# RetNet recurrence and gated MLP on one core: in the last period but one, both chunks' score products in one run, their result products in another, and one split of their rows

## The chip, the cores and the metric

The kernel runs on one core of a Trainium2 chip. The metric is the device time of one execution in microseconds (us), smaller is better. Three runs of the kernel before took 612.45, 612.64 and 613.05 us, so its median is 612.64 us. TensorE is called PE in the profile, its weight loads PEld, VectorE DVE, ScalarE ACT, GpSimd POOL and SyncE SP. PEq or SPq is an engine's sequencer, where DMAs are issued and semaphores are waited for.

## The reference, cut to what matters

```python
# attention: batch 4, 8 heads, 768 steps, head size 64; gamma has one value for each head
for t in range(S):
    state = gamma * state + outer(k[:, :, t], v[:, :, t])
    y[:, :, t] = scale * (q[:, :, t] @ state)
x = y as (3072, 512)
# MLP: w_in is 512 x 2048, w_out 2048 x 512
h = x @ w_in
g = h * erf(softplus(h))
out = g @ w_out
```

## The kernel before, in words

**Rows.** The 3072 rows are cut into 24 chunks of 128 rows, and two chunks make a group of 256, so there are 12 groups (`NG`, 0 to 11). A batch entry has 6 chunks. The recurrence is computed chunk by chunk, with half chunks of 64 rows inside, and the state is handed from half chunk to half chunk.

**One chunk of the recurrence** is made of five steps:

- `begin` (line 560): the scores, 16 products of 64x64 (line 566), and what the halves add to the state, 16 such products, or 8 for the last chunk of a batch entry, which hands on no state from its second half (line 573). A product of this size leaves two records in the trace, so these are 32 and 32 (or 16) records. The results lie in two banks of PSUM.
- `states` (line 578): on DVE, two maskings of the scores (line 582) and one or two additions to the state (line 593).
- `results` (line 595): 16 products of the states with the queries (line 611) and 16 of the masked scores with the values (line 622), into two banks; then two copies of them to the rows of x on ACT (line 630).
- `crossed_sums` (line 633): two additions on DVE (line 641) of what one half chunk owes to the other.
- `split_x` (line 643): the rows of x are split for the products in the reduced fp32 format, into hi, lo and dif (`split`, line 311: one instruction on ACT, line 314, and two on DVE, lines 315 and 316). The three go to one of three places of a ring, `XR`.

`prepare` (line 531) has transposed and scaled the queries, keys and values of two chunks some units earlier, in five steps: three on DVE, and two of eight scalings on ACT (line 550).

**The hidden layer.** Line 720 (`pair_unit`) multiplies one column block of w_in with the rows of two groups: a *unit* is 8 products of hi and lo into a first bank and 4 of dif into a second, all 128x128 weights against 512 columns. After it, `put` combines the two banks (`together`, line 320: line 322 on ACT, which reads the first bank, and line 323 on DVE, which reads the second) and sends the result to DRAM from POOL (line 731). Two sets of banks, o0/o1 and o2/o3, take turns.

**Periods.** The loop at line 1000 runs over periods `g`. `period` (line 936) gives for each the eight units, what TensorE does ahead of a unit (the first dictionary, called `pe` in the loop) and what is issued after it (the second, `other`). The order of issue for each unit is thus: `pe`, the unit's products, `other`, `put`. The order is written out by hand, and every engine works off its queue in that order. In period `g` the chunks `2g + 2` and `2g + 3` go through the recurrence, and the units multiply groups that are complete. In period 10 (`NG - 2`) these are chunks 22 and 23, and the units are those of groups 9 and 10; chunk 23 is the last of its batch entry and has the 8 products at line 573. Period 11 is the first that reads the rows of group 11 (chunks 22 and 23), from its unit 0 on. There four sets of banks take turns (r, hp, o0/o1, o2/o3).

Most periods (5 to 9 among them, line 961, and a like one at line 950) take what the helper `joined` (line 925) gives: `begin` of both chunks ahead of one unit, and `results` of both ahead of another, the first chunk in the two banks of pool `ps_h` (named hp), the second in the two of `ps_r` (named r). There `begin` stands ahead of unit 2 and `results` ahead of unit 5.

Period 10 has its own order (line 972): the four runs of small products stand ahead of units 1, 2, 3 and 5, `begin` in `ps_h` and `results` in `ps_r`. Its other work is the first of w_out: `load_w_out` (line 869, issued on SP) and `split_w_out` (line 876: line 306 on ACT, lines 307 and 308 on DVE), the load of the hidden layer back from DRAM (`load_hidden`, line 841, on SP), and `softplus`, `erf` and `gated` (lines 846, 850, 860) for the first rows.

**The output layer.** After period 12 line 905 (`project`) multiplies g with w_out, 128x128 against 512 columns, group by group. Even groups use the banks r and hp, odd ones the o banks.

Of the kernel before, what the change touches and what calls it, by code (L numbers as in the profile page):

```python
# [49 lines left out]
def kernel(  # L50
# [747 lines left out]
    a, b = JPC, JPC + 1  # L798
# [126 lines left out]
    def joined(at, to, g):  # L925

        a, b = 2 * g + 2, 2 * g + 3
        return {
            at: [(begin, a, ps_h), (begin, b, ps_r)],
            to: [(results, a, None, ps_h), (results, b, None, ps_r)],  # L930
        }
# [4 lines left out]
    def period(g, prep, next_prep):  # L936

        a, b = 2 * g + 2, 2 * g + 3
        one, two = partial(partial, unit), partial(partial, pair_unit)
        if g == G2:  # L940
            units = [one(g, n) for n in range(NPC // 2)]
            return units, {0: [(results, a), (results, b, None, ps_h)]}, {
                0: [(crossed_sums, a), (crossed_sums, b)],
                1: [(split_x, a, 2)],
                2: [(split_weights, 4)],
                3: [(steps, next_prep, 4)],
            }, range(4)
        if g < NG:
            units = [two(g - 1, ft) for ft in range(8 * (g % 2), 8 * (g % 2) + 8)]
        if g == G2 + 1:  # L950
            return units, joined(2, 5, g), {
                0: [(steps, prep)],
                1: [(split_weights, 5)],
                2: [(states, a), (states, b)],
                3: [(split_weights, 6)],
                4: [(split_weights, 7)],
                5: [(crossed_sums, a), (crossed_sums, b)],
                6: [(split_x, a, 2)],
                7: [(steps, next_prep, 1)],
            }, range(4)  # L960
        if g < NG - 2:
            return units, joined(2, 5, g), {
                0: [(steps, prep, 4)],
                1: [(convert, 2)],
                2: [(states, a), (convert, 1)],
                3: [(states, b), (convert, 1)],
                4: [(convert, 2 if g < 8 else 1)],
                5: [(crossed_sums, a), (crossed_sums, b)],
                6: [(split_x, a, 2)],
                7: [(steps, next_prep, 1 if g < NG - 3 else 4), (convert, 1)],  # L970
            }, LOADS.get(g, ())
        if g == NG - 2:
            return units, {1: [(begin, a)], 2: [(results, a)], 3: [(begin, b)], 5: [(results, b)]}, {
                0: [(steps, prep, 4), (load_w_out, 0)],
                1: [(states, a), (load_w_out, 1)],
                2: [(crossed_sums, a), (split_w_out, 0)],
                3: [(states, b), (split_x, a)],
                4: [(split_w_out, 1), (load_hiddens, 0)],
                5: [(crossed_sums, b)],
                6: [(split_x, b), (softplus, 0), (load_w_out, 2)],  # L980
                7: [(erf, 0), (gated, 0)],
            }, ()
        if g == NG - 1:
            return units, {}, {
                0: [(split_g, 0), (split_w_out, 2), (load_w_out, 3)],
                1: [(split_g, 1), (load_hiddens, 1)],
                2: [(split_w_out, 3)],
                3: [(softplus, 1), (load_w_out, 4)],
                4: [(erf, 1)],
                5: [(split_w_out, 4), (load_w_out, 5)],  # L990
                6: [(gated, 1)],
                7: [(split_g, 2), (load_hiddens, 2)],
            }, ()
        return [one(NG - 1, n) for n in range(NPC // 2)], {}, {
            0: [(split_w_out, 5), (load_w_out, 6)],
            1: [(split_g, 3), (load_w_out, 7)],
            2: [(split_w_out, 6)],
        }, ()

    for g in range(G2, NG + 1):  # L1000
        pair = load_pair(2 * g + 4) if 2 * g + 4 < NJ else iter(())
        next_prep = prepare(2 * g + 4) if 2 * g + 4 < NJ else iter(())
        units, pe, other, loads = period(g, prep, next_prep)
        for i, work in enumerate(units):
            for f, *args in pe.get(i, ()):
                f(*args)
            put = work()
            steps(pair, 3)
            for part in itertools.islice(quarters, loads.count(i)):
                load_quarter(part)  # L1010
            if g == NG - 1 and i % 2:
                W.pop(NPC // 2 + i // 2)
            if g == NG:
                W.pop(i)
            for f, *args in other.get(i, ()):
                f(*args)
            put()
            while behind:
                behind.pop(0)()
        prep = next_prep  # L1020
    split_w_out(7)

    for n in range(NG * NU):
        g, i = divmod(n, NU)
# [62 lines left out]
```

## Time and profile before

| | |
|---|---|
| median of three runs | 612.64 us (612.45 to 613.05) |
| the profiled execution | 613.15 us |
| its span, from the first instruction to the last | 611.40 us |
| around the span | 1.75 us |
| PE busy | 604.6 us, 99% of the span |
| PEld busy | 507.3 us, 83% |
| DVE busy | 459.8 us, 75% |
| ACT busy | 390.3 us, 64% |
| granted TensorE clock | 1.000 |
| period 10, from its unit 0 to unit 0 of period 11 | 286.01 to 313.05 us of the span |

A row of the timeline reads: start in us, length in us, engine, line, operation, the tile written and the tiles read, shapes, and xcount, where several records are merged. In brackets stands how long the engine was idle before it and what ended the wait. Matmuls are pipelined: a large one is listed with 0.39 us though the next starts 0.23 us later. The distance between starts is therefore what a piece of work costs PE, not the listed length.

### The profile page before, as it was taken

What the parts mean: (1) busy time and instruction counts of PE and PEld (TensorE: products, weight loads), DVE (VectorE), ACT (ScalarE), POOL (GpSimd) and SP (SyncE); (2) the same over time, 40 slices, a digit from 0 to 9 for tenths busy, and PEclk for the clock granted to TensorE, in tenths of its full rate; (3) what the DMA queues carried; (4) which work ended last, traced back from release to release, by engine and by line L of the source; (5) the groups of instructions that cost most, each with busy time, mean ns of one, the idle gap of its engine ahead of it and who ended that gap; (6) DMA issues with size and microseconds to landing.
All of it is one profiled execution on the core that took longest, in us unless ns stands there. A gap on an engine that the chain in (4) does not pass through costs nothing.

```text
span 611.4 us, 13214 instructions
## 1 busy us (share of the span) xinstructions
PE 604.6 (99%) x5222; PEld 507.3 (83%) x5222; DVE 459.8 (75%) x581; ACT 390.3 (64%) x614; POOL 132.5 (22%) x228
## 2 busy tenths in 40 slices
PE   8999999999999999999999999999999999999997
PEld 7888889888888888888788988888888888888886
DVE  5899988886978679787768978686776768668640
ACT  3667446354453634345387699889789888988920
POOL 1087435443526535241112200000000000000000
PEclk9999999999999999999999999999999999999999
DMA  9999659977979998894645834325324333531300
GB/s 203 312 263 281 149 132 248 265 161 221 219 201 277 269 270 182 243 233 151 215 143 187 286 119 148 127 70 173 103 88 154 106 129 110 172 119 55 103 35 34
DMA packets 143949, 106.28 MB, mean 174 GB/s; under 512 B 103056, under 2 KB 123792, under 8 KB 143888
## 3 DMA queue, kind: packets, MB, share of 16 engines
q1 hardware_dynamic: 128160, 58.09, 37.4%
q0 software_dynamic: 15168, 47.21, 24.6%
q8 instruction: 41, 0.67, 0.5%
q10 hardware_dynamic: 560, 0.14, 0.1%
q14 instruction: 20, 0.16, 0.1%
HBM read 69.75 MB, written 35.65 MB: 172 GB/s over the span
## 4 chain that ended last, share of the span: by engine, by line
PE 96%; SPq 2%; DMA 1%; ACT 0%; DVE 0%; issue 0%; DVEq 0%
PE o L720 31%; PE o L905 21%; PE r L905 11%; PE hp L905 11%; PE hp L665 9%; PE o L693 3%; PE hp L566 1%; DMA raw<-in_moe_w_in_dram 1%; PE hp L720 1%; PE r L720 1%; PE r L566 1%; PE r L611 1%; SPq L136 1%; PE r L622 1%; PE r L573 1%; PE hp L611 1%
## 5 line engine op out<-in xcount | busy, mean ns | idle before, releaser
L720 PE MATMUL o<-x_hi,w_hi 128*128 128x512 f32 x272 | 108.0, 397 | 0.0
L322 ACT ACTIVATE h<-o 128x512 f32<-128x512 f32 x74 | 43.8, 595 | 98.7 <-PE o L720 89.3
L720 PE MATMUL o<-x_lo,w_lo 128*128 128x512 f32 x272 | 106.0, 390 | 0.0
L860 DVE TENSOR_TENSOR e<-hid,e 128x1024 f32<-128x1024 f32 x48 | 56.7, 1222 | 61.9 <-ACT e L850 61.9
L323 DVE SCALAR_TENSOR_TENSOR h<-o,h 128x512 f32<-128x512 f32 x74 | 50.5, 686 | 34.3 <-ACT h L322 24.8
L720 PE MATMUL o<-x_dif,w_dif 128*128 128x512 f32 x272 | 72.7, 389 | 0.0
L731 POOL DMA_DIRECT2D hids<-h x72 | 39.6, 550 | 131.2 <-DVE h L323 123.1
L316 DVE SCALAR_TENSOR_TENSOR g_dif<-g_hi,g_lo 128x1024 fp32r<-128x1024 f32 x48 | 58.8, 1226 | 3.3
L720 PEld LDWEIGHTS o<-x_hi,w_hi 128*128 128x128 f32 x272 | 51.0, 188 | 11.4
L720 PEld LDWEIGHTS o<-x_dif,w_dif 128*128 128x128 f32 x272 | 51.1, 188 | 10.6
L314 ACT ACTIVATE g_hi<-e 128x1024 fp32r<-128x1024 f32 x48 | 51.0, 1062 | 13.5 <-DVE e L860 11.6
L720 PEld LDWEIGHTS o<-x_lo,w_lo 128*128 128x128 f32 x272 | 51.1, 188 | 10.1
L315 DVE TENSOR_TENSOR g_lo<-e,g_hi 128x1024 fp32r<-128x1024 f32 x48 | 58.6, 1221 | 0.5
L665 PE MATMUL hp<-xT,w 128*128 128x256 f32 x256 | 57.2, 381 | 0.0
L665 PEld LDWEIGHTS hp<-xT,w 128*128 128x128 f32 x256 | 48.0, 190 | 6.6
L846 ACT ACTIVATE e<-hid 128x1024 f32<-128x1024 f32 x48 | 48.2, 1052 | 0.3
L850 ACT ACTIVATE e<-e 128x1024 f32<-128x1024 f32 x48 | 48.2, 1052 | 0.3
L905 PE MATMUL o<-w_hi,g_hi 128*128 128x512 f32 x120 | 46.7, 389 | 0.0
L905 PE MATMUL o<-w_lo,g_lo 128*128 128x512 f32 x120 | 46.7, 389 | 0.0
L905 PE MATMUL o<-w_dif,g_dif 128*128 128x512 f32 x120 | 46.7, 389 | 0.0
L550 ACT ACTIVATE v<-v,kq_s 128x64 f32<-128x64 f32 x144 | 35.6, 335 | 0.0
L846 ACT ACT_TABLE_LOAD x24 | 30.8, 1283 | 0.5
(201 smaller groups left out, 1265.6 us busy)
## 6 DMA issues: line engine op xcount, KB each, us to landing
hids<-h POOLq DMA_DIRECT2D x72, 256.0 KB, 4.1
hid<-hids SPq DMA_DIRECT2D x36, 512.0 KB, 4.6
raw<-in_moe_w_in_dram SPq DMA_DIRECT2D x32, 256.0 KB, 5.5
raw<-in_moe_w_out_dram POOLq DMA_DIRECT2D x32, 256.0 KB, 6.2
hid<-hid SPq DMA_DIRECT2D x12, 512.0 KB, 5.2
out_dram<-y SPq DMA_DIRECT2D x23, 256.0 KB, 2.1
kb<-in_k_dram SPq DMA_DIRECT2D x144, 32.0 KB, 2.8
v<-in_v_dram POOLq DMA_DIRECT2D x18, 256.0 KB, 6.0
```

The lines of the kernel that those rows point to most:

```text
L314: nc.scalar.activation(hi, x, AF.Copy, scale=KEEP)
L315: nc.vector.tensor_tensor(lo, x, hi.bitcast(F32), op=ALU.subtract)
L316: nc.vector.scalar_tensor_tensor(dif, hi.bitcast(F32), Z, lo.bitcast(F32), op0=ALU.mult, op1=ALU.subtract)
L322: nc.scalar.activation(to, a, AF.Copy, scale=1 + 1 / Z)
L323: nc.vector.scalar_tensor_tensor(to, b, -1 / Z, to, op0=ALU.mult, op1=ALU.add)
L665: nc.tensor.matmul(HP_[ft][:, g], w[:, kk, ft % 2 * P : (ft % 2 + 1) * P], XC[g][:, kk], start=(kk == 0), stop=(kk == n_k - 1),)
L720: nc.tensor.matmul(to, W[n][i][:, kk * 2 * P + u * P : kk * 2 * P + (u + 1) * P], XR[i][:, at, kk], start=(kk == 0 and i == parts[0]), sto ...
L731: nc.gpsimd.dma_start(HID2[g][:, ft % 8], h)
L846: nc.scalar.activation(E[n], HID_[n], AF.Softplus)
L850: nc.scalar.activation(E[n], E[n], AF.Erf)
L860: nc.vector.tensor_tensor(E[n], HID_.pop(n), E[n], op=ALU.mult)
L905: nc.tensor.matmul(Y[g][t][x // 2], G[n][x][:, f, t * P : (t + 1) * P], W_OUT[ft // 2][x][:, ft % 2 * d_model : (ft % 2 + 1) * d_model], s ...
```

## The change

In period 10 the hand-written order of the recurrence is replaced by `joined(1, 3, g)`: `begin` of both chunks ahead of unit 1 and `results` of both ahead of unit 3. `states` of the second chunk moves from after unit 3 to after unit 2, both `crossed_sums` stand after unit 3, and the two splits of 128 rows (after units 3 and 6) become one of 256 rows after unit 5. By `joined` the first chunk's results lie in `ps_h` and the second chunk's scores in `ps_r`. The loads and splits of w_out, the load of the hidden layer and the activations stay after the units that they stood after.

```diff
         if g == NG - 2:
-            return units, {1: [(begin, a)], 2: [(results, a)], 3: [(begin, b)], 5: [(results, b)]}, {
+            return units, joined(1, 3, g), {
                 0: [(steps, prep, 4), (load_w_out, 0)],
                 1: [(states, a), (load_w_out, 1)],
-                2: [(crossed_sums, a), (split_w_out, 0)],
-                3: [(states, b), (split_x, a)],
+                2: [(states, b), (split_w_out, 0)],
+                3: [(crossed_sums, a), (crossed_sums, b)],
                 4: [(split_w_out, 1), (load_hiddens, 0)],
-                5: [(crossed_sums, b)],
-                6: [(split_x, b), (softplus, 0), (load_w_out, 2)],
+                5: [(split_x, a, 2)],
+                6: [(softplus, 0), (load_w_out, 2)],
                 7: [(erf, 0), (gated, 0)],
             }, ()
```

## Prediction

> **What bounds the kernel now.** I read the page first: busy times and the chain of work that ended last.
>
> ```profile
> PE 604.6 (99%) x5222; PEld 507.3 (83%) x5222; DVE 459.8 (75%) x581; ACT 390.3 (64%) x614; POOL 132.5 (22%) x228
> ...
> PE 96%; SPq 2%; DMA 1%; ACT 0%; DVE 0%; issue 0%; DVEq 0%
> ```
>
> PE is the bound: it is busy for 99% of the span, and 96% of the chain that ended last is its own work. A busy PE isn't yet a PE that only does what it must, so I asked for three stretches of equal work: periods 7, 9 and 10, each from its own unit 0 to the next period's unit 0. The columns are length, then busy time and records of PE, PEld, DVE, ACT and POOL, then clock, DMA share and GB/s.
>
> ```profile
> 207.40:233.68 26.28, 26.28 (x338) 21.80 (x337) 20.43 (x32) 12.93 (x32) 11.52 (x18) 1.00 0.94 237
> 259.73:286.01 26.28, 26.28 (x353) 21.80 (x352) 20.66 (x32) 13.78 (x39) 8.66 (x13) 1.00 0.83 217
> 286.01:313.05 27.04, 27.04 (x338) 21.80 (x336) 19.07 (x30) 14.61 (x27) 4.53 (x9) 1.00 0.47 155
> ```
>
> In all three PE has no idle time, the clock is 1.00 and PEld is busy for 21.80 us. Yet period 10 takes 27.04 us and the others 26.28. Period 7 has the very same records as period 10 (338; its second chunk too is the last of a batch entry, with half the products at line 573; period 9 has 15 more and takes no longer). Periods 7 and 9 have the joined order, period 10 has four separate runs. So 0.76 us hang on the order alone. The timeline of PE shows where. First the joined run of period 9, with the unit ahead of it and the three after it, and the first large product after the second joined run:
>
> ```profile
> 262.45 0.39 PE L720 MATMUL o<-x_hi,w_hi 128*128 128x512 f32 x1
> ...
> 265.26 0.69 PE L566 MATMUL hp<-qT,kT 64*64 64x64 f32 x32
> 265.77 0.65 PE L573 MATMUL hp<-v,kn 64*64 64x64 f32 x32
> 266.24 0.65 PE L566 MATMUL r<-qT,kT 64*64 64x64 f32 x32
> 266.71 0.65 PE L573 MATMUL r<-v,kn 64*64 64x64 f32 x32
> 267.29 0.50 PE L720 MATMUL o<-x_hi,w_hi 128*128 128x512 f32 x1
> ...
> 270.14 0.39 PE L720 MATMUL o<-x_hi,w_hi 128*128 128x512 f32 x1
> ...
> 272.86 0.39 PE L720 MATMUL o<-x_hi,w_hi 128*128 128x512 f32 x1
> ...
> 277.72 0.50 PE L720 MATMUL o<-x_hi,w_hi 128*128 128x512 f32 x1
> ```
>
> A plain unit takes 272.86 - 270.14 = 2.72 us. The unit ahead of a run and the run together take 267.29 - 262.45 = 4.84, and the unit after it 270.14 - 267.29 = 2.85. A joined run thus costs 4.84 + 2.85 - 2 x 2.72 = 2.25 us. The second joined run, that of the results, comes to 277.72 - 272.86 = 4.86 with its unit, 0.02 more. Together they make the period: 8 x 2.72 + 2.25 + 2.27 = 26.28. Now the first separate run of period 10, and the period's end:
>
> ```profile
> 286.01 0.39 PE L720 MATMUL o<-x_hi,w_hi 128*128 128x512 f32 x1
> ...
> 288.83 0.69 PE L566 MATMUL hp<-qT,kT 64*64 64x64 f32 x32
> 289.34 0.65 PE L573 MATMUL hp<-v,kn 64*64 64x64 f32 x32
> 289.92 0.50 PE L720 MATMUL o<-x_hi,w_hi 128*128 128x512 f32 x1
> ...
> 313.05 0.39 PE L720 MATMUL r<-x_hi,w_hi 128*128 128x512 f32 x1
> ```
>
> A separate run takes 289.92 - 288.83 = 1.09 us, where a joined one of twice the work takes 267.29 - 265.26 = 2.03. To enter it costs 288.83 - 286.01 - 2.72 = 0.10, and the first large products after it lose 0.13 as above, so one is 1.32 us. Four are 4 x 1.32 = 5.28 us, and 8 x 2.72 + 5.28 = 27.04, which is the whole period.
>
> **The change part by part.**
>
> *PE.* The two kernels issue the same products; their instruction lists differ on PE in the order and the banks alone. Four runs become two. Inside a run 64 records cost 266.24 - 265.26 = 0.98 at the start and 0.94 on average (2.03 - 1.09), so of each removed run 1.32 - 0.94 = 0.38 us goes: what it costs to enter, to leave, and to start anew. Two times 0.38 is 0.76 us. The direct reading is the same: period 10 becomes a period 7, 27.04 to 26.28. Chunk 23's 16 records at line 573 don't change this, as period 7 has them in a joined run. Were they to gain from the joining after all, it would be at most half of their 0.47 us, 0.24 more.
>
> Weighed against a rule: the Trainium skill, page "TensorEngine Tiling (Array Packing)", section "Instruction Overhead", gives each matmul about 60 cycles, whatever its free size below that. If that were all that a run costs, the count of matmuls (equal before and after) would fix the price and the gain would be 0. The rows above speak against it, since twice the records take 2.03 and not 2.18 us, and entry and exit come on top.
>
> *The wait that draws nearer.* With two units between `begin` and `results`, where the other periods have three, the second chunk's states could come late. They stand on DVE behind line 323 of unit 1.
>
> ```profile
> 292.07 0.60 ACT L322 ACTIVATE h<-o 128x512 f32<-128x512 f32 x1 [3.44 <-PE o L720]
> ...
> 293.03 0.69 DVE L323 SCALAR_TENSOR_TENSOR h<-o,h 128x512 f32<-128x512 f32 x1 [1.20 <-PE o L720]
> ...
> 298.72 0.75 DVE L582 TENSOR_TENSOR am<-hp,causal_d 128x256 f32<-128x256 f32 x2
> 299.38 0.41 DVE L593 TENSOR_TENSOR state<-state,hp 128x256 f32<-128x256 f32 x1
> ```
>
> After the change unit 1 starts at 286.01 + 4.84 = 290.85, 0.93 later than before, and unit 2 at 293.70. Line 323 moves to 293.96 and ends at 294.65; the states take 299.79 - 298.72 = 1.07 and end near 295.7. The results start at 293.70 + 2.81 = 296.51, those of the second chunk 0.98 later, at 297.49. That leaves 1.8 us of room, so I cost the wait at nothing. The second chunk's scores, now two units earlier, need its scaled values:
>
> ```profile
> 285.80 2.01 ACT L550 ACTIVATE v<-v,kq_s 128x64 f32<-128x64 f32 x8
> ```
>
> They are there at 287.81; the first product that reads them (line 573 for chunk 23) would come near 289.81 + 0.47 = 290.3. This too is costed at nothing.
>
> *DVE and ACT.* Two splits of 128 rows become one of 256. The rows are the whole-group split of period 9 and the two small ones of period 10:
>
> ```profile
> 280.36 1.06 ACT L314 ACTIVATE x_hi<-xT 128x1024 fp32r<-128x1024 f32 x1
> ...
> 281.45 1.22 DVE L315 TENSOR_TENSOR x_lo<-xT,x_hi 128x1024 fp32r<-128x1024 f32 x1
> ...
> 296.60 0.62 ACT L314 ACTIVATE x_hi<-xT 128x512 fp32r<-128x512 f32 x1
> ...
> 307.39 0.62 ACT L314 ACTIVATE x_hi<-xT 128x512 fp32r<-128x512 f32 x1
> 308.04 1.28 ACT L846 ACT_TABLE_LOAD   x1
> ...
> 304.75 0.50 PE L720 MATMUL o<-x_hi,w_hi 128*128 128x512 f32 x1
> 309.20 0.69 DVE L316 SCALAR_TENSOR_TENSOR x_dif<-x_hi,x_lo 128x512 fp32r<-128x512 f32 x1
> ```
>
> The last split is ready at 309.89 now, for period 11 at 313.05. In the new order units 3 and 4 start at 293.70 + 4.86 = 298.56 and at 301.41, unit 5 at 304.13, and period 11 at 312.29. The split follows `put` of unit 4, whose line 322 starts 2.15 after the unit does (292.07 against 289.92 above) and line 323 3.11: near 304.5, or a little later behind the split of w_out, say 305.3. Then 2 x 1.22 on DVE make it ready near 307.7, by 4.6 us in time. The work saved (4 x 0.69 - 2 x 1.22 = 0.3 us on DVE) lies under PE and is worth nothing by itself. But with no split between them, the activations start right after line 322 of unit 5: that moves by the 0.62 that unit 5 comes earlier (it started at 304.75), and the table load by 0.65 more, the distance from the small split's start at 307.39 to 308.04, to 306.77. The chain behind it (softplus, erf, gate, splits of w_out) so comes 1.27 us earlier, where PE comes 0.76 earlier: it gains room.
>
> *Queues.* POOL and SP have the same instructions in the same order. The SP load of the third pair of w_out is released when the second pair is split, behind unit 3, which comes 298.56 - 297.99 = 0.57 later:
>
> ```profile
> 297.99 0.50 PE L720 MATMUL o<-x_hi,w_hi 128*128 128x512 f32 x1
> 303.31 12.49 SPq L871 DMA_DIRECT2D w<-wof  x2
> 316.47 1.05 ACT L306 ACTIVATE x_hi<-w 128x1024 fp32r<-128x1024 f32 x1
> ```
>
> From 303.31, the first of the two issues, to the use at 316.47 lie 13 us. No DMA is added.
>
> *Does the gain last to the end?* The waits of PE that the trace lists are four groups in the opening stage, 2.9 us in all, the first of them
>
> ```profile
> PE o L417 <- POOL ident masks.py:199: 1.5, 1, 1.5
> ```
>
> After that PE waits for nobody, so what matters is who is nearly late. The tightest place that I find is the first `project`, which needs the bank hp that line 323 empties:
>
> ```profile
> 326.81 7.38 SPq L871 DMA_DIRECT2D w<-wof  x2
> 330.46 1.06 ACT L306 ACTIVATE w_hi<-w 128x1024 fp32r<-128x1024 f32 x1 [0.46 <-DMA w<-wof]
> 345.95 0.68 DVE L323 SCALAR_TENSOR_TENSOR h<-hp,h 128x512 f32<-128x512 f32 x1
> ...
> 347.48 0.39 PE L905 MATMUL hp<-w_dif,g_dif 128*128 128x512 f32 x1
> ```
>
> The bank is free at 346.63, 0.85 us before its product. DVE works almost without a break from 331.55 to that point, and what started it is the load issued at 326.81. That load waits for a split on DVE that belongs to the chain which comes 1.27 earlier, so the room should grow to about 1.36.
>
> *Sum.* The profiled execution took 613.15 us (span 611.40 and 1.75 around it): 613.15 - 0.76 = 612.39. It lies 0.51 above the median of the runs, 612.64, from which the same step gives 611.88. I forecast **611.9 us**, 0.12% less.
>
> **The rivals.**
>
> *Price by count* (no gain). Runs cost what their products cost, wherever they stand. For it: 0.98 of the 1.09 us is there for the first 64 records of the joined run too. Against it: two joined periods, at 26.28 each. Time: 612.64.
>
> *A wait takes the gain in part.* If the states of chunk 23 end over 1.8 us late, at 297.49, each further microsecond goes to PE; with 0.4 the time is 612.3. Against it: line 323 of unit 1 waits for PE alone and stands ahead of the states; the split of w_out stands behind them.
>
> *Slower: the load of the fifth pair of w_out* (326.81 above) lands late. From 326.81 to the split at 330.46 it now takes 3.65 us. Moved with its chain, it decides from 3.65 + 1.36 = 5.01 us on, and the kernel is slower than before from 5.01 + 0.76 = 5.77.
>
> ```profile
> DMA to landing us min/median/max: 3.3/3.7/6.2
> ```
>
> The eight loads of this line took 3.3 to 6.2, median 3.7. With the slowest, PE waits 6.2 - 5.01 = 1.19 us: 612.64 - 0.76 + 1.19 = 613.07. Against it: the load moves with its neighbours, so it meets the same traffic, and the DMA share is falling (0.94, 0.83, 0.47 in the stretches above).
>
> **How the numbers follow.** Forecast (gain 0.5 to 1.0): 0.76. By count: 0.06. Wait in part: 0.05. Slower by the load: 0.04. Slower by more, or more than 1.2 gained, for a reason that I don't see: 0.04 and 0.05. The range reaches down to 612.64 - 1.00 (with the 0.24) less the 0.19 by which the lowest run lies under the median, and a little more, 611.3; and up past the case by count to 612.9, as the runs alone spread over 0.60. A measurement of this kernel can tell about 0.2% from no change, 1.2 us; the forecast lies inside. Faster by over 0.2% needs under 611.41: 0.06, the last case and the edge of the forecast. Slower needs over 613.87, more than the load gives: 0.05, nearly all from the unseen. Within: 0.89.
>
> **What would show it.** In the profile after, period 10 has two runs of 2.0 us, and lasts 26.28 us from its unit 0 to the next period's; PE has no idle ahead of line 611; line 593 of chunk 23 ends near 295.7; the first activation table of the period loads near 306.8; the first row of line 905 stands 0.76 earlier than at 346.32. An idle PE ahead of the second chunk's line 611, or line 905 at 346.32 again, would prove me wrong, and so would a joined run of 2.2 us or more.

## The result, and the profile after

The kernel after takes 612.03 us (median of 22 runs, 611.72 to 612.29). The kernel before, measured beside it in 22 runs, takes 612.82 us (612.34 to 614.45). The ratio is 0.9986, with a 95% interval of 0.998 to 0.9992: 0.79 us less, where 0.76 were forecast. The profiled execution of the kernel after took 612.18 us, its span is 610.5 us.

The first view is the one on which the forecast rested, of the kernel after: period 10, the stretch from there to the first `project` (line 905), and from there to the last products. Columns as before: length, then busy time and records of PE, PEld, DVE, ACT and POOL, clock, DMA share, GB/s.

```profile
285.82:312.10 26.28, 26.28 (x337) 21.80 (x336) 18.58 (x28) 15.03 (x27) 4.86 (x9) 1.00 0.45 160
312.10:345.37 33.27, 33.27 (x193) 29.53 (x192) 30.28 (x31) 21.69 (x28) 5.40 (x10) 1.00 0.66 225
345.37:605.61 260.24, 260.24 (x1150) 215.48 (x1149) 177.64 (x161) 208.13 (x203) 1.62 (x3) 1.00 0.34 111
```

And the last two stretches of the kernel before:

```profile
313.05:346.32 33.27, 33.27 (x193) 29.53 (x192) 29.99 (x31) 22.31 (x29) 5.74 (x11) 1.00 0.67 226
346.32:606.56 260.24, 260.24 (x1150) 215.55 (x1149) 177.94 (x162) 208.11 (x203) 1.62 (x3) 1.00 0.34 111
```

Period 10 went from 27.04 to 26.28 us. Behind it each stretch is as long as before, 33.27 and 260.24 us, with no idle time on PE: the gain is made in period 10 and handed on whole to the end. The remaining 0.19 us of the difference between the two traces lies ahead of period 10, which starts at 285.82 in place of 286.01, in code that is the same in both. It differs from one execution to the next: with that same code period 10 starts at 285.74, 285.93 and 285.79 us in three of the kernels below.

The timeline of PE in the new period 10, one row for each unit's start and each group of small products:

```profile
285.82 0.39 PE L720 MATMUL o<-x_hi,w_hi 128*128 128x512 f32 x1
...
288.63 0.69 PE L566 MATMUL hp<-qT,kT 64*64 64x64 f32 x32
289.15 0.65 PE L573 MATMUL hp<-v,kn 64*64 64x64 f32 x32
289.62 0.65 PE L566 MATMUL r<-qT,kT 64*64 64x64 f32 x32
290.08 0.64 PE L573 MATMUL r<-v,kn 64*64 64x64 f32 x16
290.65 0.50 PE L720 MATMUL o<-x_hi,w_hi 128*128 128x512 f32 x1
...
296.32 0.69 PE L611 MATMUL hp<-qT,state 64*64 64x64 f32 x32
296.83 0.65 PE L622 MATMUL hp<-am,v 64*64 64x64 f32 x32
297.30 0.67 PE L611 MATMUL r<-qT,state 64*64 64x64 f32 x32
297.77 0.67 PE L622 MATMUL r<-am,v 64*64 64x64 f32 x32
298.37 0.50 PE L720 MATMUL o<-x_hi,w_hi 128*128 128x512 f32 x1
```

Two runs of 290.65 - 288.63 = 2.02 and 298.37 - 296.32 = 2.05 us stand where there were four of 1.09. No row has an idle time in brackets. Now DVE and ACT of the kernel after, at the place where a wait could have come up and where the activations begin:

```profile
293.76 0.69 DVE L323 SCALAR_TENSOR_TENSOR h<-o,h 128x512 f32<-128x512 f32 x1 [2.14 <-PE o L720]
294.37 0.75 DVE L582 TENSOR_TENSOR am<-r,causal_d 128x256 f32<-128x256 f32 x2
295.04 0.41 DVE L593 TENSOR_TENSOR state<-state,r 128x256 f32<-128x256 f32 x1
...
306.35 1.23 DVE L316 SCALAR_TENSOR_TENSOR x_dif<-x_hi,x_lo 128x1024 fp32r<-128x1024 f32 x1
...
306.57 1.28 ACT L846 ACT_TABLE_LOAD   x1
```

The states of chunk 23 end at 295.45, 1.85 us ahead of the second chunk's results at 297.30. The split is ready at 307.58, the first table load starts at 306.57.

### The profile page after: what moved, and what is told of

The parts are those of the page before. It is cut to its first block, busy times and chain, and to the rows that moved or that the text cites. A ratio compares the mean times of both kernels' runs of the same rounds, so it can differ in the third digit from the quotient of the medians.

```text
span 610.5 us, 13210 instructions
## 1 busy us (share of the span) xinstructions
PE 603.9 (99%) x5222; PEld 507.6 (83%) x5222; DVE 459.3 (75%) x579; ACT 390.3 (64%) x613; POOL 132.1 (22%) x228
## 4 chain that ended last, share of the span: by engine, by line
PE 96%; SPq 2%; DMA 1%; ACT 0%; DVE 0%; issue 0%; DVEq 0%
PE o L720 31%; PE o L905 21%; PE r L905 11%; PE hp L905 11%; PE hp L665 9%; PE o L693 3%; PE r L566 1%; DMA raw<-in_moe_w_in_dram 1%; PE hp L720 1%; PE r L720 1%; PE r L573 1%; PE hp L611 1%; PE hp L566 1%; SPq L136 1%; PE r L611 1%; PE hp L622 1%
```

## The experiments

The theory: a run of small products that stands between large ones costs TensorE a fixed 0.38 us beside its products (29 ns for each 64x64 product in a run), so the number of runs is what counts. Each experiment below starts from the kernel after. Runs of the kernel before stood beside each one.

### The split taken apart again

```diff
-                5: [(split_x, a, 2)],
-                6: [(softplus, 0), (load_w_out, 2)],
+                5: [(split_x, a)],
+                6: [(split_x, b), (softplus, 0), (load_w_out, 2)],
```

Expected: 

> The kernel after, with its one split of 256 rows cut in two of 128 again (behind units 5 and 6); the runs of small products stay joined. Handover theory (each run taken out of TensorE's row of large products saves 0.38 us): nothing changes for TensorE, period 10 takes 26.28 us, the time stays that of the kernel after, 0.76 us under the kernel before. Rival (the gain comes from the merged split and the activations that start earlier): the gain is gone, the time is that of the kernel before, and only the first table load of period 10 moves back, by some 0.6 us, under either theory.

Measured: 612.06 us (11 runs) against 612.89 for the kernel before, ratio 0.9987 (0.9978 to 0.9995), the same as the kernel after. Period 10 and the first table load of this run:

```profile
285.74:312.02 26.28, 26.28 (x337) 21.80 (x336) 18.88 (x30) 14.61 (x27) 4.53 (x9) 1.00 0.45 160
```
```profile
307.01 1.28 ACT L846 ACT_TABLE_LOAD   x1
```

26.28 us again, with DVE busy for 0.30 us more (18.88 against 18.58). The table load starts 307.01 - 285.74 = 21.27 us into the period, where it was 306.57 - 285.82 = 20.75 in the kernel after: 0.52 later, and it costs nothing. So the merged split has no part in the gain.

### Only the scores joined

```diff
-            return units, joined(1, 3, g), {
+            return units, {1: [(begin, a, ps_h), (begin, b, ps_r)], 3: [(results, a, None, ps_h)],
+                           5: [(results, b, None, ps_r)]}, {
...
-                3: [(crossed_sums, a), (crossed_sums, b)],
+                3: [(crossed_sums, a)],
...
-                5: [(split_x, a, 2)],
-                6: [(softplus, 0), (load_w_out, 2)],
+                5: [(crossed_sums, b)],
+                6: [(split_x, a, 2), (softplus, 0), (load_w_out, 2)],
```

Expected: 

> Only the scores of the two chunks are joined (ahead of unit 1, banks as in the kernel after); the results stand ahead of units 3 and 5, in two runs. Three runs in period 10. Handover theory: half the gain, period 10 takes 26.28 + 0.38 = 26.66 us, the time is 0.38 us under the kernel before. Rival by split or by banks (what pays is one split, or the use of the banks hp and r in turn): the whole gain, 26.28 us and 0.76 us.

Measured: 612.76 us (11 runs) against 612.89, ratio 0.9995 (0.9987 to 1.0004). That is 0.13 us less, where 0.38 was expected, and the times alone don't tell 0.38 us from none. The period does:

```profile
285.93:312.58 26.65, 26.65 (x338) 21.78 (x336) 18.68 (x28) 14.10 (x26) 4.32 (x8) 1.00 0.45 157
```

26.65 us, half way between 27.04 and 26.28, with one split and the banks of the kernel after. So neither of these pays, but each of the two runs that are gone, 0.37 to 0.39 us.

### Four runs in each of the periods 4 to 9

```diff
-            return units, joined(2, 5, g), {
+            return units, {2: [(begin, a, ps_h)], 3: [(begin, b, ps_r)], 4: [(results, a, None, ps_h)],
+                           5: [(results, b, None, ps_r)]}, {
                 0: [(steps, prep, 4)],
```

Expected: 

> The kernel after with periods 4 to 9 taken apart instead: four runs of small products ahead of units 2, 3, 4 and 5, the same banks, splits and places of DVE work as before. Handover theory: each of the six periods goes from 26.28 to 27.04 us, 6 x 0.76 = 4.56 us more than the kernel after, so about 616.6 us, 0.6% slower than the kernel before. Price by count, or a cause that is special to period 10: 612.0 us, the six periods at 26.28.

Measured: 616.71 us (5 runs) against 612.89, ratio 1.0061 (1.0047 to 1.0075). Four of the six periods, 4, 6, 7 and 9, in this kernel:

```profile
128.19:155.22 27.03, 27.03 (x337) 21.80 (x336) 20.50 (x31) 12.93 (x32) 11.14 (x17) 1.00 0.79 206
182.03:209.07 27.04, 27.04 (x354) 21.81 (x352) 21.88 (x33) 11.78 (x30) 14.28 (x23) 1.00 0.97 263
209.07:236.10 27.03, 27.03 (x337) 21.80 (x336) 20.23 (x32) 12.92 (x32) 11.51 (x18) 1.00 0.91 226
262.91:289.95 27.04, 27.04 (x354) 21.81 (x352) 20.57 (x32) 13.80 (x39) 8.66 (x13) 1.00 0.83 210
```

(Periods 5 and 8 have a chunk that begins a batch entry, with fewer products, and are shorter in every kernel.) Taken apart, these periods cost what period 10 did. The medians differ by 616.71 - 612.03 = 4.68 us, where 4.56 was expected. The traces are finer: the six periods take 289.95 - 128.19 = 161.76 us here and 285.82 - 128.57 = 157.25 in the kernel after, 4.51 more, or 0.38 for each of twelve more runs. The cost has nothing to do with period 10.

### The room ahead of the results

```diff
-                2: [(states, b), (split_w_out, 0)],
+                2: [(split_w_out, 0), (states, b)],
```

Expected: 

> The kernel after with the states of the second chunk put behind the first split of w_out in DVE's order of unit 2. In the trace of the kernel after they end at 295.45 and the second chunk's results start at 297.30, 1.85 us of room; the split's two instructions take 2.45 us. If the room is as read: TensorE waits some 0.5 to 0.7 us ahead of the second chunk's results, period 10 takes about 26.9 us, and the gain is nearly gone (0.1 to 0.3 us under the kernel before). If results do not hang on these states so closely: no wait, 26.28 us.

Measured: 612.99 us (11 runs) against 612.89, ratio 1.0002 (0.9993 to 1.0011): the gain is gone. DVE of this kernel, and the second half of the results on PE:

```profile
296.75 0.75 DVE L582 TENSOR_TENSOR am<-r,causal_d 128x256 f32<-128x256 f32 x2
297.42 0.41 DVE L593 TENSOR_TENSOR state<-state,r 128x256 f32<-128x256 f32 x1
```
```profile
296.29 0.69 PE L611 MATMUL hp<-qT,state 64*64 64x64 f32 x32
...
297.65 0.96 PE L611 MATMUL r<-qT,state 64*64 64x64 f32 x29 [0.20 <-PE hp L622]
...
298.45 0.68 PE L622 MATMUL r<-am,v 64*64 64x64 f32 x31
299.06 0.50 PE L720 MATMUL o<-x_hi,w_hi 128*128 128x512 f32 x1
```

The states end at 297.83. The results of the second chunk start late and are drawn out: the run lasts 299.06 - 296.29 = 2.77 us in place of 2.05, so 0.72 us are lost, of 0.5 to 0.7 expected. Period 10 lasts from 285.79 to 312.80, 27.01 us, where some 26.9 was expected and the kernel before takes 27.04. Note how the view names the wait: only 0.20 us appear as idle time, and they are put down to PE's own row before (line 622), which ends at 296.81 + 0.65 = 297.46, where the idle time starts. What was changed is the order of DVE, and the run goes on as DVE lets it: it starts behind the maskings, which end at 297.50, and its first row is drawn out to 0.96 us, across the end of the states. (The second chunk's results use the states and go into the banks r, which these DVE rows read.) The time lies 0.10 above the kernel before, where 0.1 to 0.3 below was expected; the interval is wider than that difference. The rival of the prediction that a wait takes the gain is thus a real mechanism, and 1.85 us of room kept it out.

### One more joining, in the opening

In the opening, chunk 4's results and chunk 5's scores stand one hidden block apart, between products of 128x128 weights and 256 columns in full fp32 (line 665).

```diff
-        6: [(scale_early, b, 0), (results, a, ("o0", "o1")), (T, b, None, ("o2", "o3")), (steps, pair), (block_scales,)],
-        7: [(crossed_sums, a), (begin, b, ps_r), (split_weights, 0)],
+        6: [(scale_early, b, 0), (T, b, None, ("o2", "o3")), (steps, pair), (block_scales,)],
+        7: [(results, a, ("o0", "o1")), (begin, b, ps_r), (split_weights, 0), (crossed_sums, a)],
```

Expected: 

> The kernel after with one more joining, in the opening: the results of chunk 4 wait from hidden block 6 to block 7 and share a run with the scores of chunk 5, so one run of small products fewer. Handover theory: 0.38 us less than the kernel after, 1.14 us under the kernel before, if the opening's products of 128 x 256 columns in full fp32 pay for entering and leaving a run as the units do. If the cost belongs to the units' reduced format or their 512 columns, the gain is another, between 0 and 0.38. If DVE, which converts weights there with hardly a break, becomes late by the moved work, TensorE waits in the opening and the gain is gone.

Measured: 611.70 us (11 runs) against 612.81, ratio 0.9983 (0.9974 to 0.9992): 1.11 us under the kernel before, and the fastest version here. Its lead of some 0.3 us over the kernel after lies inside the intervals; the traces show it. First the kernel after, then this one:

```profile
42.60 0.69 PE L566 MATMUL r<-kqT 64*64 64x64 f32 x32
...
56.88 0.64 PE L573 MATMUL r<-v,kq 64*64 64x64 f32 x16
57.45 7.17 PE L665 MATMUL hp<-xT,w 128*128 128x256 f32 x32
```
```profile
42.41 0.69 PE L566 MATMUL r<-kqT 64*64 64x64 f32 x32
...
56.39 0.64 PE L573 MATMUL r<-v,kq 64*64 64x64 f32 x16
56.96 7.17 PE L665 MATMUL hp<-xT,w 128*128 128x256 f32 x32
```

From chunk 4's scores (42.60 and 42.41) to the products behind chunk 5's (57.45 and 56.96) there are 14.85 us in the one and 14.55 in the other: 0.30 of the 0.38 expected. There the run that went was followed by transposes and not by large products; whether that makes the difference of 0.08 was not tried. DVE did come later in this trace: its weight conversion behind chunk 4's states goes on at 52.37 us in place of 50.67, after 1.86 us of idle time that the view puts down to a DMA of `v`. Whether the new order brought that about was not tried; TensorE waited for nothing in this stretch.

### Probes between two units

What is it that a run costs? Two kernels put small products, whose results nobody reads, ahead of units 0 and 7 of periods 5 to 8. These kernels do more work than the reference asks for, and only their traces are used. The cut is from the second.

```diff
+    def probe(g, i):
+        to = [ps_h.tile([P, HP, C], F32, name="hp") for _ in range(2)]
...
+                    nc.tensor.matmul(to[n][at, u, :D], ident[own, :D], causal[own, :D], start=True, stop=True)
...
             for f, *args in pe.get(i, ()):
                 f(*args)
+            if 5 <= g <= 8 and i in (0, 7):
+                probe(g, i)
             put = work()
```

The first: 

> The kernel after with a probe between two units in periods 5 to 8, whose result nobody reads: ahead of unit 0 one product of 128x128 weights against 64 columns, ahead of unit 7 four products of 64x64 weights (periods 5 and 6, full fp32, operands as the identity and the causal mask) or two of 64x128 (periods 7 and 8, the reduced fp32 format, operands of the units). The cost of a probe is the distance of the units around it less 2.72 us. Theory that the change of the array's tiling costs: the 64x64 and 64x128 probes cost 0.38 us and their own products (some 0.12 us by 29 ns for each), some 0.5, in both formats, and the 128x128 probes only their own product, under 0.2. Theory that the change of the number format costs: the full fp32 probes cost some 0.4 to 0.5 in both shapes, those in the reduced format under 0.2 in both.

The second: 

> The kernel after with other probes at the same places, results unread. Periods 5 and 7: ahead of unit 0 two products of 128x128 weights against 64 columns in the reduced format, ahead of unit 7 two of 64x128 in full fp32. Periods 6 and 8: ahead of unit 0 one product of 64x64 in full fp32, ahead of unit 7 sixteen of them. If a run of another tiling has a fixed price of 0.38 us and 29 ns for each 64x64 product, the one costs 0.41 and the sixteen 0.85 us (four took 0.50). If it is the count that costs, one takes a quarter of four's 0.50, some 0.13, and sixteen 2.0. The 128x128 pair, without a change of tiling, costs its own exposed weight loads alone, 0.17 to 0.25; the 64x128 pair with the change some 0.45 to 0.55.

The cost of a probe is the distance between the starts of the units around it, less 2.72 for each unit. Where another probe stands in place of the next unit, the distance is taken to its start; to enter a probe of another tiling costs 0.09, and where that is the next one, these 0.09 are counted to it and not to the probe ahead. One of each, read from PE in the first kernel (the four products of 64x64, then one of 128x128, both in full fp32):

```profile
175.60 0.39 PE L720 MATMUL o<-x_hi,w_hi 128*128 128x512 f32 x1
...
178.41 0.34 PE L953 MATMUL hp<-causal,ident 64*64 64x64 f32 x8
178.69 0.50 PE L720 MATMUL o<-x_hi,w_hi 128*128 128x512 f32 x1
...
181.54 0.33 PE L944 MATMUL hp<-causal,ident 128*128 128x64 f32 x2
181.68 0.48 PE L720 MATMUL o<-x_hi,w_hi 128*128 128x512 f32 x1
...
184.51 0.39 PE L720 MATMUL o<-x_hi,w_hi 128*128 128x512 f32 x1
```

The four: 181.54 - 175.60 - 2 x 2.72 = 0.50. The one: 184.51 - 181.54 - 2.72 = 0.25. Each probe stands in two periods and gave the same within 0.01:

| probe | tiling changes | format changes | cost, us | expected |
|---|---|---|---|---|
| 1 of 64x64, full fp32 | yes | yes | 0.48 | 0.41 |
| 4 of 64x64, full fp32 | yes | yes | 0.50 | 0.5 |
| 16 of 64x64, full fp32 | yes | yes | 0.85 | 0.85 |
| 2 of 64x128, full fp32 | yes | yes | 0.59 | 0.45 to 0.55 |
| 2 of 64x128, reduced | yes | no | 0.43 | some 0.5 |
| 1 of 128x128, full fp32 | no | yes | 0.25 | under 0.2 |
| 1 of 128x128, reduced | no | no | 0.14 | under 0.2 |
| 2 of 128x128, reduced | no | no | 0.24 | 0.17 to 0.25 |

The sixteen are read from these rows of the second kernel: 209.46 - 203.17 - 2 x 2.72 = 0.85.

```profile
203.17 0.39 PE L720 MATMUL o<-x_hi,w_hi 128*128 128x512 f32 x1
...
205.98 0.69 PE L952 MATMUL hp<-causal,ident 64*64 64x64 f32 x32
...
209.46 0.30 PE L943 MATMUL hp<-x_hi,w_hi 128*128 128x64 f32 x2
```

From 4 to 16 products 0.35 us are added, 29 ns each, and from 16 to the 32 of a real run (1.32) another 0.47, again 29 ns each. What remains at none is 0.38 us. Three rows lie above what was expected: the single 64x64 product, the two of 64x128 in full fp32, and the one of 128x128 in full fp32. The first is taken up at the end. The third leaves two records, for which the expectation did not allow. For the second there is no row to compare.

The format is not it: two products in the reduced format cost 0.24, as much as one in full fp32, which leaves two records as well. The change of the array's tiling is. Rows that differ in it and agree in format and records cost 0.48 against 0.25 (one product in full fp32) and 0.43 against 0.24 (two in the reduced format), so 0.23 and 0.19 us go with the change of tiling alone. The weight loads show it as well, in the second kernel (sixteen of 64x64, and behind the next unit two of 128x128).

```profile
205.98 0.56 PEld L952 LDWEIGHTS hp<-causal,ident 64*64 64x64 f32 x32 [0.35 <-issue]
209.24 0.41 PEld L943 LDWEIGHTS hp<-x_hi,w_hi 128*128 128x128 f32 x2
```

And in the kernel before, ahead of the first separate run of period 10:

```profile
288.82 0.56 PEld L566 LDWEIGHTS hp<-qT,kT 64*64 64x64 f32 x32 [0.35 <-issue]
```

Ahead of every probe with another tiling the weight loads stand still for 0.35 us, as they do there; ahead of the 128x128 ones they don't. The Trainium skill, page "TensorEngine Tiling (Array Packing)", section "Key Properties", says that a change of the tiling mode, and not of the tile alone, drains TensorE. The rows agree with it; the price, which the page doesn't give, is theirs. Not all of the 0.38 need be the drain: a short product costs 0.14 (a single one in the reduced format) even where the tiling stays. By the two pairs 0.19 to 0.23 us go with the tiling; how the rest of the 0.38 divides was not measured by itself.

## Why the prediction was right, point by point

- **What bounds the kernel.** PE was the bound and had no wait behind the opening; both are so in the kernel after, where the waits of PE are the same four groups of the opening. That is why 0.76 us of PE are 0.76 us of the kernel. The first `project` starts at 345.37 in place of 346.32, 0.95 earlier: 0.76 from period 10 and the 0.19 from ahead of it.
- **The sum of the PE step**, 2 x 0.38: period 10 took 26.28 us, to the hundredth. The step was sound because periods 7 and 9 of the same kernel already showed the new order. The experiments add what the prediction could only infer: one run less gives half (26.65), twelve more cost 4.51 us, and probes of 4 and 16 products lie on the line that starts at the same 0.38.
- **The extra 0.24 for chunk 23's products** at line 573, an end of the range, didn't come: its 16 records take 0.57 us to the next product (290.08 to 290.65), as the 32 of period 9 do (266.71 to 267.29, 0.58). The reason that fits the kernel is that half the products is not half the time where they lie on half of the array's four 64x64 tiles. Line 573 leaves out the second half chunk, and with it the tiles of its rows, so the other two tiles still take four products each. Where all four tiles have less to do, time does go. Line 611 has 8 products instead of 16 for a chunk that begins a batch entry, two on each tile, and they take 0.28 us in period 8 of the kernel after, where the 16 of the new period 10 take 296.83 - 296.32 = 0.51:

```profile
249.43 0.46 PE L611 MATMUL hp<-qT,state 64*64 64x64 f32 x16
249.71 0.65 PE L622 MATMUL hp<-am,v 64*64 64x64 f32 x32
```

- **The wait that draws nearer.** Forecast: states end near 295.7, 1.8 us of room. In the trace 295.45 and 1.85; the period starts 0.19 earlier, so this is within 0.1. By the fourth experiment the room is real: 2.45 us more ahead of the states cost 0.72, where the room of 1.85 leaves 0.60 of them.
- **DVE, ACT and queues at nothing.** Right; the first experiment takes the merged split back at no cost. The table load came at 306.57, forecast 306.77, or 306.58 with the same shift of 0.19. The split was ready at 307.58 (forecast 307.7). The chain behind it came earlier than PE did, as forecast: the bank hp was free ahead of `project` by

```profile
344.67 0.68 DVE L323 SCALAR_TENSOR_TENSOR h<-hp,h 128x512 f32<-128x512 f32 x1
...
346.53 0.39 PE L905 MATMUL hp<-w_dif,g_dif 128*128 128x512 f32 x1
```

 1.18 us (346.53 - 344.67 - 0.68), up from 0.85. The forecast said 1.36; the other 0.18 went on ACT. The table load of the second `softplus` came 0.70 us earlier and not 1.46 (1.27 and the shift), as it now waits for the load of the hidden layer (line 841), whose issue moved from 317.77 to 316.83 only. The split of the fifth pair of w_out then starts behind ACT's own work and 1.26 earlier, where it waited for its DMA before. First the kernel before, then two rows of the kernel after:

```profile
322.41 1.28 ACT L846 ACT_TABLE_LOAD   x1
```
```profile
321.71 1.28 ACT L846 ACT_TABLE_LOAD   x1 [0.89 <-DMA hid<-hid]
...
329.20 1.05 ACT L306 ACTIVATE w_hi<-w 128x1024 fp32r<-128x1024 f32 x1
```

- **One reading of the queues** was wrong, without cost. The load of the third pair of w_out was to be released by the split of the second pair (line 307) and so to come 0.57 us later, near 303.9. It was issued at 298.01, 5.3 us earlier than in the kernel before: its wait now ends with the second chunk's results (line 611).
- **The rivals.** Price by count is refuted by the third experiment and by the probes (a single product costs 0.48, not the 0.13 of a quarter of four). The wait in part has its mechanism but not its occasion. The late load did not come: the eight loads took 3.2 to 6.2 us, median 3.6, and the split of the fifth pair no longer waits for its own.
- **The level.** 611.9 was reckoned from a median of 612.64 over three runs; over 22 the kernel before stands at 612.82, and 612.82 - 0.76 = 612.06 is within 0.03 of what was measured.

## What to carry to other kernels

Where TensorE never waits, look for time that it spends on itself: compare stretches of equal products, and a difference in their length with equal clock and no idle time was a matter of order here. Small products in another tiling should stand together, since each run of them between full-size ones costs 0.38 us here beside its products, whether it has four of them or thirty-two. Before joining them, find the one result that now comes due sooner, and the queue in which it stands: a split's two DVE instructions, 2.45 us, ahead of it gave the whole gain back.

## What was not expected of the hardware

- One 64x64 product costs as much as four on the four tiles of the array (0.48 and 0.50 us with the fixed part), whereas from four to thirty-two each adds 29 ns. The expected 0.41 for one was too low by 0.07. All of these fit one rule, worked out here from the rows: 0.38 us, and 0.117 (four times 29 ns) for each product on the tile that has most of them. That gives 0.50 for one product as for one on each tile, 0.85 for four on each, and 1.32 for the eight on each of a real run, and no gain from chunk 23's two idle tiles. It was found afterwards; no experiment varied the products of one tile alone.
- Joining two products of 64 columns to units of the same tiling and format is not free: 0.14 us for the first and 0.10 for the second, though 64 columns are an eighth of a large product's 512, which take 0.23, so 0.03 by that rate (an estimate). The trace suggests why: behind a single one that starts at 208.57 us in the first kernel of probes, the next load of 128x128 weights starts at 208.58 and lasts 0.19 us, longer than those 0.03. That this is the whole cost was not tried.
